# Issuing the first batch's Newton products twice and moving up the first output products in a fused attention and gated-network kernel

## The chip, the core and the metric

The kernel runs on one core of a Trainium2 chip. The metric is device time in microseconds (us) of one execution, in runs of one program; less is better. A core has TensorE (PE, with its weight loads as a separate row, PEld), VectorE (DVE), ScalarE (ACT), GpSimd (POOL) and the queue of SyncE (SP), which here issues nearly all loads. Matmul results land in PSUM, which has eight banks.

## What is computed

Nyström attention over 4 batches, 8 heads, 576 rows and 64 columns, then two gated layers (512 to 1536 to 512) over the 2304 rows. Cut to what matters:

```python
q_lm, k_lm = means of 18 consecutive rows: 32 landmarks per head
A, Bm, C = softmax(q k_lm^T), softmax(q_lm k_lm^T), softmax(q_lm k^T)
Z = Bm.T / (norm1(Bm) * norminf(Bm) + 1e-6)
for _ in range(6):
    Z = 2 * Z - Z @ Bm @ Z            # Newton rounds, 32x32 per head
x = A @ Z @ C @ v
g = x @ w_gate; x = (g * sigmoid(g) * (x @ w_val)) @ w_out     # layer 1
x = (sigmoid(x @ w_gate2) * (x @ w_val2)) @ w_out2             # layer 2
```

## The kernel before

The attention output is never formed. For each batch b, `front(b, g)` (g is one half of the heads) takes the landmark means (`lm`), transposes k and q on TensorE (`tp`, `lt`), and forms the three softmaxes (`cs` and `e` for C, `bm` and `bs` for Bm, `as` and `sx` for A) and C·v (`cv`). `back(b)` normalises Bm and runs the Newton rounds. A round is eight products of 32x32 by 32x96, one for each head, made by `prod` (L273 to L278) into the tile `nw`, and one update on DVE (L283 for the first round, L288 for five, L294 for the last), which makes the next `rw`. After seven such products the result is transposed (`ut`, L297) and copied to `UT`.

Layer 1 goes over six chunks c of 256 hidden columns. `uw_steps` (word U) multiplies `UT[b]` by the chunk's gate and value weights (`pu`), and splits the result into two parts (`uw`, L360 on ACT, L361 on DVE). `gv1_steps` (word G) multiplies that by A (`pg`, `pv`), applies SiLU on ACT (L453), multiplies on DVE (L455), and splits again (`hh`, `hl`). `o1_steps` (word O) multiplies by the output weights (`po`); for c = 0 the sum is copied by ACT (`acc`, L479), later it is added by DVE (L481). Layer 2 follows, from about 620 us on.

The weights come in as raw 32-bit pieces (`raw`, three buffers, loaded by SP in order with the loads of q, k and v). Each piece is converted by two ACT instructions (L324, L327) and two DVE instructions (L329, L333); an output piece (`wo`) also takes a cast on ACT (L360) and a subtraction on DVE (L361). A chunk has four pieces for gate and value and two for the output.

The order in which this is written out is a list of words, `first` (L589 to L592). F, B, U, G and O are the steps above; `I0` and `I1` convert chunk 0 or 1 up to its fourth piece, which U needs; `J0` and `J1` go on to its sixth, which O needs. While a U, G or O word is written out, the weight conversion advances by one step after each of its steps. The framework's scheduler then sets each engine's queue, with the written order as priority, so that instructions of neighbouring words mix. Each engine works through its queue strictly in that order. ACT loads a table (ACT_TABLE_LOAD) each time it changes between the exponentials of a front and SiLU.

PSUM has four groups of banks: `gv` 3, `n` 1 (`nw`, `ut`), `o` 2, `a` 2. The matmuls of `nw` write one bank.

Of the kernel before, what the change touches and what calls it, by code (L numbers as in the profile page):

```python
# [14 lines left out]
def nystrom_moe_kernel(tc, q, k, v, wg1, wv1, wo1, wg2, wv2, wo2, out):  # L15
    nc = tc.nc
    B, H, S, D = q.shape
    M = 32
    P = 128
# [23 lines left out]
    def ptile(shape, tag, name):  # L43
        return psum.tile(shape, F32, tag=tag, name=name, bufs=PB[tag])
# [16 lines left out]
    def mm(o, l, r, start=True, stop=True):  # L61
        nc.tensor.matmul(o, l, r, start=start, stop=stop, skip_group_check=True)  # L62
# [19 lines left out]
    def flat(x):  # L82
        return x.rearrange("p a b -> p (a b)")
# [6 lines left out]
    def step(fill, n=1):  # L90
        while n and fill:
            try:
                next(fill[0])
                n -= 1
            except StopIteration:
                fill.pop(0)
# [4 lines left out]
    def small(tag, shape, nm_, bufs=2):  # L101
        return att.tile(shape, F32, tag=tag, name=f"{tag}{nm_}", bufs=bufs)

    def pst(b, shape, nm, g=0):

        tag = "n" if nm in ("nw", "ut") else "a"
        if b == 0:
            tag = {"tp": "gv", "cs": "o", "as": "o"}.get(nm, tag)
        return ptile(shape, tag, f"{nm}_{b}_{g}")
# [113 lines left out]
    def a_steps(b, g):  # L223
        s = SX[b, g]
        asm = small("asm", [P, L], f"{b}_{g}")
        nc.vector.tensor_reduce(asm, s, axis=AX.X, op=ALU.add)
        nc.vector.tensor_scalar(asm, asm, 1e-9, None, op0=ALU.add)
        nc.vector.reciprocal(asm, asm)
        yield
        nc.vector.tensor_tensor(s, s, asm[:, :, None].to_broadcast([P, L, M]), op=ALU.mult)  # L230
        yield
        at = flat(small("sx", [P, L, M], f"{b}_{g}t", 3))
        nc.vector.transpose(out=at, in_=flat(s))
        hi, lo = AH[:, 8 * g + b], AH[:, 8 * g + 4 + b]
        nc.scalar.copy(hi, at)
        nc.vector.tensor_tensor(lo, at, hi.bitcast(F32), op=ALU.subtract)
        AT[b, g, 0] = hi
        AT[b, g, 1] = lo
        yield

    def back(b):

        def sm(tag, shape, bufs=2):
            return small(tag, shape, b, bufs)

        bs, bsm, BC = BS[b]

        nc.vector.tensor_scalar(bsm, bsm, 1e-9, None, op0=ALU.add)
        nc.vector.reciprocal(bsm, bsm)
        nc.vector.tensor_tensor(bs, bs, bsm[:, :, None].to_broadcast([P, 2, M]), op=ALU.mult)  # L250
        nc.scalar.copy(BC[:, :, 0:M], bs)

        bmt = sm("bmt", [P, 2, M])
        nc.vector.transpose(out=flat(bmt), in_=flat(bs))
        nrm = sm("nrm", [P, 2, 2])
        nc.vector.tensor_reduce(nrm[:, 0], bs, axis=AX.X, op=ALU.add)
        nc.vector.tensor_reduce(nrm[:, 1], bmt, axis=AX.X, op=ALU.add)
        yield
        nb = sm("nb", [P, 4, M], 1)
        nc.vector.tensor_copy(nb, nrm.rearrange("p a b -> p (a b)")[:, :, None].to_broadcast([P, 4, M]))  # L260
        nbt = sm("nbt", [P, 4, M], 1)
        nc.vector.transpose(out=flat(nbt), in_=flat(nb))
        nmax = sm("nmax", [P, 2, 2])
        nc.vector.tensor_reduce(flat(nmax), nbt, axis=AX.X, op=ALU.max)
        rr = sm("rr", [P, 2])
        nc.vector.tensor_tensor(rr, nmax[:, 0], nmax[:, 1], op=ALU.mult)
        nc.vector.tensor_scalar(rr, rr, 1e-6, None, op0=ALU.add)
        nc.vector.reciprocal(rr, rr)
        yield


        def prod(x):
            ps = pst(b, [P, 2, 96], "nw")  # L273
            for g in range(2):
                for h in range(4):
                    hs = slice(M * h, M * h + M)
                    mm(ps[hs, g], x[hs, g, 0:M], x[hs, g])
            return ps  # L278

        ga = [a_steps(b, g) for g in range(2)]  # L280
        ps = prod(BC)
        RW = sm("rw", [P, 2, 96], 2)
        nc.vector.tensor_tensor(RW, ps, rr[:, :, None].to_broadcast([P, 2, 96]), op=ALU.mult)  # L283
        yield
        for it in range(5):
            ps = prod(RW)
            RW2 = sm("rw", [P, 2, 96], 2)
            nc.vector.scalar_tensor_tensor(RW2, RW, 2.0, ps, op0=ALU.mult, op1=ALU.subtract)  # L288
            RW = RW2
            step(ga)  # L290
            yield
        ps = prod(RW)
        UU = flat(sm("rw", [P, 2, 96], 2))[:, 0:P].rearrange("p (g d) -> p g d", g=2)
        nc.vector.scalar_tensor_tensor(UU, RW[:, :, M:], 2.0, ps[:, :, M:], op0=ALU.mult, op1=ALU.subtract)  # L294
        yield
        ps = pst(b, [P, P], "ut")
        nc.tensor.transpose(ps, flat(UU), ident)  # L297
        nc.vector.tensor_copy(flat(UT[b]), ps)
        yield
        while ga:  # L300
            step(ga)
            yield
# [273 lines left out]
    def emit(word, nw=1):  # L576
# [10 lines left out]

    wfill.extend(weights(0, c) for c in range(2))
    first = (  # L589
        "F00 F01 B0 I0 F10 U00 G00 J0 F11 I1 U10 B1 O00 G10 J1 F20 O10 U01 G01 "  # L590
        "F21 U11 B2+F30 O01 G11 F31 U02 O11 G02 B3 U12 O02 G12 U03 O12 G03 U13 O03 G13"
    )  # L592
    for w in first.split():
# [78 lines left out]
```

## Time and profile before

| | us |
|---|---|
| median of 3 runs | 907.71 (906.84 to 910.90) |
| profiled execution | 907.64 |
| its span, first to last instruction | 905.9 |
| TensorE busy | 872.2 (96%), mean granted clock 0.991 |
| VectorE busy | 523.4 (58%) |
| ScalarE busy | 396.3 (44%) |
| TensorE busy in the first 110 us | 84.47, mean granted clock 0.92 |

The profiled execution is 0.07 us under the median. A granted clock of 1.00 is 2.4 GHz, of 0.50 is 1.2 GHz; a stretch with a value between holds both. Busy shares over the whole span say little here: the last three quarters are bound by TensorE, and what can be lost or won lies in the first 110 us, where fronts, Newton rounds and weight conversions compete for all engines.

### The profile page before, as it was taken

The page shows a single profiled execution, that of the slowest core. Times are in us where ns is not written, and L with a number is a line of the kernel's source. Part 1 is how long each engine was busy: PE and PEld are TensorE (multiplying, and loading weights), DVE is VectorE, ACT ScalarE, POOL GpSimd, SP SyncE. Part 2 cuts the span into 40 slices and gives each one's busy share as a digit, 9 for nine tenths or more (in the row PEclk, how much of TensorE's full clock was granted, in tenths as well). Part 3 has the DMA queues.
Part 4 walks back from the last instruction along what each step waited for, and adds up shares of the span by engine and source line. Part 5 has one row for each costly group of instructions (what it writes and reads, how often), then busy time and mean ns, then how long its engine had stood idle before and what let it go on. Part 6 is the DMA issues. An engine that isn't in the chain of part 4 may idle for free.

```text
span 905.9 us, 16181 instructions
## 1 busy us (share of the span) xinstructions
PE 872.2 (96%) x6604; PEld 744.0 (82%) x6604; DVE 523.4 (58%) x1079; ACT 396.3 (44%) x845; POOL 55.8 (6%) x90
## 2 busy tenths in 40 slices
PE   5778999999999999999999999999999999999997
PEld 4456777789999999999988888888888888888886
DVE  4977665765977678769861153355347236433342
ACT  5688477755653355537643262143125114111111
POOL 4530323000000000000000000000000000000000
PEclk9898999999999999999999999999999999999999
DMA  8666221011611132203010031012004000000132
GB/s 270 178 201 195 80 78 30 3 52 43 177 52 52 48 94 71 71 4 114 24 47 1 1 101 39 1 52 88 1 1 139 1 1 24 1 1 0 47 94 71
DMA packets 27083, 57.68 MB, mean 64 GB/s; under 512 B 4224, under 2 KB 7296, under 8 KB 27008
## 3 DMA queue, kind: packets, MB, share of 16 engines
q1 hardware_dynamic: 25280, 54.28, 20.1%
q10 hardware_dynamic: 1728, 2.36, 1.1%
q8 instruction: 52, 0.85, 0.4%
q14 instruction: 23, 0.19, 0.1%
HBM read 51.90 MB, written 4.72 MB: 63 GB/s over the span
## 4 chain that ended last, share of the span: by engine, by line
PE 89%; DVE 4%; ACT 4%; issue 1%; DMA 1%; SPq 0%; ACTq 0%; DVEq 0%
PE po L62 33%; PE pv L62 24%; PE pg L62 24%; PE pu L62 3%; PE tp L145 1%; PE nw L62 1%; PE cs L62 1%; ACT L453 1%; DMA raw<-in_moe_w_val_dram 1%; PE as L62 1%; PE cv L62 1%; DVE lm L131 0%; DMA kin<-in_k_dram 0%; ACT e L172 0%; PE et L195 0%
## 5 line engine op out<-in xcount | busy, mean ns | idle before, releaser
L62 PE MATMUL po<-hh,wo 128*128 128x288 f32 x768 | 164.9, 303 | 1.4 <-ACT acc L479 0.9
L62 PE MATMUL po<-wo,h 128*128 128x512 f32 x648 | 152.2, 389 | 0.0
L526 DVE TENSOR_TENSOR hf<-hf,pv 128x512 f32<-128x512 f32 (+1 forms) x60 | 38.1, 634 | 194.2 <-PE pv L62 194.2
L62 PEld LDWEIGHTS po<-wo,h 128*128 128x128 f32 x648 | 121.1, 188 | 25.3 <-ACT h L360 0.3
L62 PEld LDWEIGHTS po<-hh,wo 128*128 128x128 f32 x768 | 124.4, 188 | 17.1 <-issue 12.9
L62 PE MATMUL pg<-AH,w 128*128 128x512 f32 (+1 forms) x480 | 136.1, 368 | 0.0
L62 PE MATMUL pv<-AH,w 128*128 128x512 f32 (+1 forms) x480 | 136.0, 368 | 0.0
L62 PE MATMUL po<-hl,wo 128*128 128x288 f32 x384 | 113.5, 297 | 0.0
L525 ACT ACTIVATE hf<-pg 128x512 f32<-128x512 f32 (+1 forms) x60 | 33.2, 553 | 165.7 <-PE pg L62 152.1
L62 PE MATMUL pg<-AH,uw 128*128 128x288 f32 x576 | 100.0, 299 | 0.5 <-ACT uw L360 0.5
L62 PE MATMUL pv<-AH,uw 128*128 128x288 f32 x576 | 97.6, 300 | 2.6 <-ACT sg L453 2.6
L62 PEld LDWEIGHTS pg<-AH,w 128*128 128x128 f32 x480 | 87.3, 188 | 15.5
L62 PEld LDWEIGHTS pv<-AH,w 128*128 128x128 f32 x480 | 87.0, 189 | 15.0
L360 ACT CAST h<-hf 128x512 fp32r<-128x512 f32 (+1 forms) x60 | 34.6, 576 | 124.2 <-DVE hf L526 124.2
L62 PEld LDWEIGHTS pg<-AH,uw 128*128 128x128 f32 x576 | 83.7, 188 | 5.5 <-issue 3.4
L62 PEld LDWEIGHTS pv<-AH,uw 128*128 128x128 f32 x576 | 83.3, 190 | 5.6 <-ACT sg L453 3.1
L547 DVE TENSOR_TENSOR oacc<-po,oacc 128x512 f32<-128x512 f32 x90 | 61.9, 691 | 41.0 <-PE po L62 39.9
L62 PE MATMUL pg<-x1l,w 128*128 128x512 f32 x192 | 74.7, 389 | 0.0
L62 PE MATMUL pv<-x1l,w 128*128 128x512 f32 x192 | 74.7, 389 | 0.0
L62 PEld LDWEIGHTS po<-hl,wo 128*128 128x128 f32 x384 | 72.2, 188 | 0.7 <-DVE uw L361 0.5
L481 DVE TENSOR_TENSOR acc<-po,acc 128x288 f32<-128x288 f32 x128 | 56.4, 454 | 16.1 <-PE po L62 15.6
L324 ACT ACTIVATE cv<-raw 128x512 f32<-128x512 f32 x72 | 48.5, 674 | 26.5 <-DVE cv L333 11.3
(121 smaller groups left out, 1092.1 us busy)
## 6 DMA issues: line engine op xcount, KB each, us to landing
raw<-in_moe_w_out_dram SPq DMA_DIRECT2D x24, 512.0 KB, 4.0
raw<-in_moe_w_gate_dram SPq DMA_DIRECT2D x48, 128.0 KB, 3.2
raw<-in_moe_w_val_dram SPq DMA_DIRECT2D x48, 128.0 KB, 3.2
raw<-in_moe_w_gate_dram SPq DMA_DIRECT2D x24, 256.0 KB, 3.0
raw<-in_moe_w_val_dram SPq DMA_DIRECT2D x24, 256.0 KB, 3.4
kin<-in_k_dram SPq DMA_DIRECT2D x8, 576.0 KB, 4.4
qin<-in_q_dram SPq DMA_DIRECT2D x8, 576.0 KB, 5.5
vin<-in_v_dram SPq DMA_DIRECT2D x8, 576.0 KB, 5.5
```

What stands on the lines that cost most here:

```text
L62: nc.tensor.matmul(o, l, r, start=start, stop=stop, skip_group_check=True)
L145: nc.tensor.transpose(ps[:, j], flat(src[:, 2 * u:2 * u + 2]), ident)
L324: nc.scalar.activation(t0, hiw.bitcast(F32), AF.Copy, scale=2.0 ** -112)
L360: nc.scalar.copy(hi, x)
L453: nc.scalar.activation(sg, pss[0], AF.Silu)
L481: nc.vector.tensor_tensor(sl, ps, sl, op=ALU.add)
L525: nc.scalar.activation(h, pss[0], AF.Sigmoid)
L526: nc.vector.tensor_tensor(h, h, pss[1], op=ALU.mult)
L547: nc.vector.tensor_tensor(acc, ps, acc, op=ALU.add)
```

## The change

Two things. First, for batch 0 `prod` issues its eight products twice, the second time into further columns of the same `nw` tile (five groups of 96 columns wide, within one bank), which nothing reads. Second, in the list of words `F11`, `J0` and `O00` move ahead of `B1` and `I1`.

```diff
         def prod(x):
-            ps = pst(b, [P, 2, 96], "nw")
-            for g in range(2):
-                for h in range(4):
-                    hs = slice(M * h, M * h + M)
-                    mm(ps[hs, g], x[hs, g, 0:M], x[hs, g])
-            return ps
+            ps = pst(b, [P, 5 if b == 0 else 2, 96], "nw")
+            for o in range(0, 4 if b == 0 else 2, 2):
+                for g in range(2):
+                    for h in range(4):
+                        hs = slice(M * h, M * h + M)
+                        mm(ps[hs, o + g], x[hs, g, 0:M], x[hs, g])
+            return ps[:, 0:2]
...
-        "F00 F01 B0 I0 F10 U00 G00 J0 F11 I1 U10 B1 O00 G10 J1 F20 O10 U01 G01 "
+        "F00 F01 B0 I0 F10 U00 G00 F11 J0 O00 B1 I1 U10 G10 J1 F20 O10 U01 G01 "
```

In the built programs TensorE's semaphore is raised once for each round, on its last product: after the eighth before, after the sixteenth now. The update on DVE waits for that, so for batch 0 it now stands behind the second eight products as well.

On TensorE, the Newton rounds of batch 0 stand among the transposes and `cs` products of the next batch's front. Before:

```order
L62 MATMUL nw_0_476<-rw_474 32x96 x8
L145 MATMUL tp_0_667<-ident,qin_0_147 128x128 x3
L145 MATMUL tp_0_672<-ident,qin_0_147 128x128 x3
L62 MATMUL nw_0_491<-rw_485 32x96 x8
L145 MATMUL tp_0_677<-ident,qin_0_147 128x128 x3
L62 MATMUL cs_0_691<-kq_0_635,bdq_0_663 32x288
L62 MATMUL nw_0_503<-rw_500 32x96 x8
```

Now, at the same place on TensorE:

```order
L62 MATMUL nw_0_484<-rw_482 32x96 x16
L135 MATMUL lt_0_717<-ident,lm_0_709 128x128
L145 MATMUL tp_0_723<-ident,qin_0_147 128x128 x3
L62 MATMUL nw_0_507<-rw_501 32x96 x16
L145 MATMUL tp_0_728<-ident,qin_0_147 128x128 x3
L145 MATMUL tp_0_733<-ident,qin_0_147 128x128 x3
L62 MATMUL cs_0_747<-kq_0_691,bdq_0_719 32x288
L62 MATMUL nw_0_527<-rw_524 32x96 x16
```

Each round has sixteen products, and three transposes moved from ahead of the third round to behind it.

On ACT, from the casts of the first `uw` to the first SiLU of G00 (`pg` to `sg`, behind its table load). Before:

```order
L360 CAST uw_0_0_817<-pu_0_0_803 128x512
L196 COPY eT_0_718<-et_0_719 96x384
L360 CAST uw_0_1_821<-pu_0_1_804 128x512
L184 ACTIVATE bs_684,bsm_685<-bs_684 128x32
L196 COPY eT_0_718<-et_0_724 96x384
L327 ACTIVATE cv_855<-raw 128x512
L324 ACTIVATE cv_935<-raw 128x512
L327 ACTIVATE cv_936<-raw 128x512
L360 CAST wo_0_564<-cv_855 128x512
L453 ACT_TABLE_LOAD
L453 ACTIVATE sg_0_0_841<-pg_0_0_827 128x288
```

Now, from the same front's `bs` exponential on:

```order
L184 ACTIVATE bs_740,bsm_741<-bs_740 128x32
L196 COPY eT_0_774<-et_0_775 96x384
L196 COPY eT_0_774<-et_0_780 96x384
L362 CAST wo_0_620<-cv_675 128x512
L326 ACTIVATE cv_991<-raw 128x512
L362 CAST uw_0_0_873<-pu_0_0_859 128x512
L362 CAST uw_0_1_877<-pu_0_1_860 128x512
L362 CAST wo_0_620<-cv_911 128x512
L329 ACTIVATE cv_992<-raw 128x512
L455 ACT_TABLE_LOAD
L455 ACTIVATE sg_0_0_897<-pg_0_0_883 128x288
```

The front's exponential and copies and one weight conversion moved ahead of the `uw` casts; behind them, ahead of the table load, stand two instructions where there were six.

On TensorE, from the last product of G00 on (`pv_0_0_911` before, `pv_0_0_967` now): the transposes of F11, then before:

```order
L145 MATMUL tp_1_994<-ident,qin_1_328 128x128 x3
L62 MATMUL cs_1_1005<-kq_1_952,bdq_1_980 32x288 x4
L62 MATMUL cs_1_1011<-kq_1_952,bdq_1_980 32x288 x4
L62 MATMUL pu_0_1_1156<-w_1_933,ut_82 32x512
L62 MATMUL pu_0_0_1155<-w_1_933,ut_82 32x512
```

And now:

```order
L145 MATMUL tp_1_1045<-ident,qin_1_328 128x128 x3
L62 MATMUL po_0_0_1193<-hh_0_0_901,wo_0_620 128x288 x2
L62 MATMUL po_0_0_1193<-hl_0_0_902,wo_0_620 128x288
L145 MATMUL tp_1_1050<-ident,qin_1_328 128x128 x3
L62 MATMUL cs_1_1061<-kq_1_1008,bdq_1_1036 32x288 x4
L62 MATMUL po_0_0_1193<-hh_0_0_932,wo_0_620 128x288
L62 MATMUL cs_1_1067<-kq_1_1008,bdq_1_1036 32x288 x4
L62 MATMUL po_0_0_1193<-hh_0_0_932,wo_0_620 128x288
L62 MATMUL po_0_0_1193<-hl_0_0_933,wo_0_620 128x288
L62 MATMUL po_0_0_1211<-hh_0_0_901,wo_0_620 128x288 x2
```

The products of U10 (`pu`), which need four converted pieces of chunk 1, stood right behind F11's `cs`; now all 48 `po` products of O00, the rest of F11 and the first Newton round of batch 1 stand ahead of them. The last 4382 of TensorE's 5662 products have the same order in both programs.

## Rows read from the trace of the kernel before

**Rows 1.** Busy time by stretch of the span; columns in the first line.

```profile
core 0: us, PE busy (x) PEld busy (x) DVE busy (x) ACT busy (x) POOL busy (x), PEclk, DMA share, GB/s
28.60:32.00 3.40, 1.59 (x9) 0.98 (x9) 3.40 (x7) 2.31 (x6) 3.09 (x6) 1.00 1.03 263
32.00:38.60 6.60, 5.89 (x63) 3.49 (x67) 6.23 (x11) 4.79 (x11) 5.33 (x7) 0.50 0.46 139
38.60:44.60 6.00, 3.06 (x63) 1.42 (x63) 5.89 (x14) 3.03 (x5) 0.00 (x0) 0.98 0.44 138
57.90:62.70 4.80, 4.78 (x25) 4.40 (x25) 3.67 (x8) 3.95 (x11) 0.82 (x2) 0.65 0.42 115
62.70:70.25 7.55, 3.20 (x26) 1.32 (x26) 5.10 (x9) 5.97 (x13) 4.49 (x6) 0.95 0.82 281
70.25:76.40 6.15, 6.15 (x67) 3.35 (x71) 3.22 (x8) 5.47 (x15) 0.00 (x0) 0.50 0.58 172
76.40:86.30 9.90, 8.95 (x160) 8.08 (x156) 9.07 (x29) 7.15 (x17) 0.00 (x0) 1.00 0.76 186
57.90:88.20 30.30, 24.98 (x283) 19.06 (x284) 22.66 (x55) 24.22 (x55) 5.31 (x8) 0.83 0.67 193
86.30:97.20 10.90, 10.20 (x146) 8.28 (x145) 8.12 (x16) 5.50 (x12) 4.01 (x6) 1.00 0.19 57
97.20:210.00 112.80, 109.44 (x1455) 89.23 (x1452) 74.80 (x193) 77.45 (x170) 19.52 (x32) 1.00 0.20 57
210.00:620.00 410.00, 410.00 (x2737) 366.43 (x2737) 260.18 (x542) 192.06 (x414) 0.00 (x0) 1.00 0.19 57
```

**Rows 2.** Who TensorE waited for, 26 to 100 us: total, times, longest.

```profile
PE pu L62 <- DVE w L333: 4.6, 2, 3.5
PE pv L62 <- ACT sg L453: 2.1, 1, 2.1
PE po L62 <- ACT acc L479: 0.9, 1, 0.9
```

**Rows 3.** TensorE in order of time: start, us, instruction, [idle before <-releaser].

```profile
32.71 0.86 PE L62 MATMUL nw<-rw 32*32 32x96 f32 x16 [1.91 <-DVE rw L283]
...
37.70 0.86 PE L62 MATMUL nw<-rw 32*32 32x96 f32 x16
38.49 1.31 PE L62 MATMUL cs<-kq,bdq 128*32 128x288 f32 x14
...
42.27 0.53 PE L62 MATMUL nw<-rw 32*32 32x96 f32 x16 [1.00 <-DVE rw L288]
43.22 0.33 PE L297 MATMUL ut<-ident,rw 128*128 128x128 f32 x1 [0.41 <-DVE rw L294]
44.62 1.09 PE L62 MATMUL pu<-w,ut 64*32 64x512 f32 x16 [1.08 <-DVE w L333]
...
90.17 0.53 PE L62 MATMUL nw<-rw 32*32 32x96 f32 x16
90.63 0.93 PE L62 MATMUL pg<-AH,uw 128*128 128x288 f32 x5
```

**Rows 4.** ACT in order of time, same columns.

```profile
46.86 0.60 ACT L360 CAST uw<-pu 128x512 fp32r<-128x512 f32 x1
...
50.08 0.69 ACT L327 ACTIVATE cv<-raw 128x512 uint32<-128x512 uint32 x1
51.31 0.62 ACT L360 CAST wo<-cv 128x512 fp32r<-128x512 f32 x1 [0.54 <-DVE cv L333]
51.94 1.28 ACT L453 ACT_TABLE_LOAD   x1
53.24 0.41 ACT L453 ACTIVATE sg<-pg 128x288 f32<-128x288 f32 x1
...
57.93 0.41 ACT L453 ACTIVATE sg<-pg 128x288 f32<-128x288 f32 x1
...
88.21 0.41 ACT L453 ACTIVATE sg<-pg 128x288 f32<-128x288 f32 x1
```

## The prediction, before the result was known

> **What bounds the kernel now.** I read the busy time by stretch first. From 210 to 620 us TensorE is busy in all of 410.00 us, and from 97 to 210 us in 109.44 of 112.80 at full clock [rows 1]. So whatever TensorE has gained or lost when it gets there stays to the end, as long as the work behind is the same; the last 4382 of its products stand in the same order in both programs. The case is decided ahead of 97 us.
>
> There the reader should see three losses. From 32 to 38.6 us the clock is at 0.50, that is 1.2 GHz, while TensorE is busy for 5.89 of 6.60 us [rows 1]; this is the Newton stretch of batch 0. From 62.7 to 70.25 us TensorE is busy for 3.20 of 7.55 us, and the longest wait of all lies there: `pu` of U10 waits 3.5 us for the last piece of chunk 1's weights (`w`, L333) [rows 1, 2]. Then from 70.25 to 76.4 us it works without a gap, but at 0.50 [rows 1]. Over 57.9 to 88.2 us, from one SiLU of G00 to the first of G10, TensorE is busy 24.98 us at a mean clock of 0.83, ACT 24.22 and DVE 22.66, of 30.30 [rows 1, 4]. No engine is full: 24.98 x 0.83 is 20.7 us of TensorE work at full clock, so some 9.6 us are lost to waits and to the low clock.
>
> **Part 1, the doubled products.** Eight products take 0.79 us from their start to that of the next work at the low clock (37.70 to 38.49) and 0.46 at the full one (90.17 to 90.63) [rows 3]. The added ones do not run beside the update of their own round, since it waits for the sixteenth product. So a round gets longer by one of these two times. The first is free: its products end before 28 us, and its update (`rw`, L283) comes only just ahead of 32.71, behind other DVE work [rows 3]. Rounds 2 to 4 fall in the low-clock stretch, 5 to 7 behind it: 3 x 0.79 + 3 x 0.46 = 3.8 us on the way to `ut`, if nothing hides it. Some of it is hidden: DVE is busy for 6.23 of 6.60 and 5.89 of 6.00 us there, and the late rounds waited for it (1.00 and 0.41 us) [rows 1, 3]. That DVE work can run while the second eight run, as far as the queue's order lets it. The least is therefore 3.8 - 1.4 = 2.4 us. I take 2.6, nearer to the low end, because DVE was full. `ut` then starts at 45.8 instead of 43.22, and `pu` of U00, which waited for weights until 44.62 and not for `ut` [rows 3], starts at about 46.5: 1.9 late.
>
> Who waits for that? G00's first SiLU. Before, the first `uw` cast starts at 46.86 and the table load only at 51.94, because six instructions stood between the second cast and the load, among them a `wo` cast that waited 0.54 us for DVE [rows 4]. Now `pu` ends at 46.5 + 1.1 = 47.6; ACT ends a conversion (until 48.3), makes two `uw` casts (0.5 each), a `wo` cast (0.6), a conversion (0.7, of the 0.69 in [rows 4]) and the load (1.28): 51.9 us, against 53.24. I take -1.2 us at G00's SiLUs, since the second SiLU follows through the same two table loads. Bounds: -2.5 (all of the lateness hidden) and +1 (`pu` 3.8 late and a DVE wait on top).
>
> **Part 2, the moved words.** The 48 `po` products of O00 now come into the wait for chunk 1's weights, and U10 comes behind them. TensorE's wait of 3.5 us for `w` goes, and the 0.9 us that `po` waited for an `acc` copy [rows 2] becomes a wait among other work. What is next? ACT. Its work of the stretch is the same but for the ends: two `kq` copies and two `bdk` scalings come in ahead of G10's first SiLU, and one pair of conversions (2 x 0.69 [rows 4]) goes behind it, which I take as equal. So ACT's 24.2 us [rows 1] is the floor, 6.1 under the 30.3 of before. It won't be reached: the exponentials of F11 and the `bm` product, whose bank they free, still follow each other, and the last `uw` cast waits for `pu`. I give these 1.2 us, half of what the same kind of waits on TensorE's side comes to in [rows 2] (2.1). That makes -4.9 us; bounds -6.1 (ACT never waits) and -2 (two thirds of its waits stay, which were for copies and transfers and not for `pu`).
>
> SP matters here as well: in the new order the second `val` load of chunk 1's fourth piece stands ahead of F11's `kin` load and not behind it, so it no longer queues behind a load that waits for transposes. I cost this at nothing; it is part of why the `w` wait goes.
>
> At G10's first SiLU the new order has run four Newton rounds of batch 1 where the old one has run one, and some five more transposes, with four `pv` and `pg` products left over. Transposes and products are alike in time (0.93 us for five products [rows 3], so below 0.2 each): 3 x 0.46 and one product more, 1.5 us less to do. TensorE is busy 10.20 of 10.90 us from 86.3 on [rows 1], so nearly all of it counts: -1.5; bounds 0 and -2.5.
>
> **The sum.** -1.2 - 4.9 - 1.5 = -7.6 us, against the profiled execution's 907.64, which is 0.07 under the median: 900.0 us. The bounds together, +1 - 2 + 0 and -2.5 - 6.1 - 2.5, give 906.6 and 896.5.
>
> **A rule on the clock.** TensorE ran transposes and one product of two columns from 28.6 to 32.0 us, 1.59 of 3.40 us, and the clock was at 0.50 behind it; from 38.6 to 44.6 us it was busy for about the same share, 3.06 of 6.00, with Newton and `cs` products among it, and the clock stayed at 0.98 [rows 1]. The Trainium skill, "TensorE: Matmul & The Clock Gate", Part 1 (the clock gate), says that the low clock is the default and that activity of the engine releases it. By that rule the second eight products, which fill gaps with activity, should bring the clock up sooner in the Newton stretch; the rows agree in that the clock did come back after a busy stretch, and do not show whether so few more products are enough.
>
> **The rivals.**
> Clock back early, as a mechanism of this kernel: the added products lift the clock at the third round instead of behind the fourth. Two rounds of sixteen then take 0.92 instead of 1.58 us each, and half of the low-clock `cs` time (1.31 us [rows 3]) is saved: 1.3 + 0.7 = 2.0 us. For it: the two rows above. Against: in 32.0 to 38.6 us TensorE was busy for nine tenths and the clock still came back only at the end [rows 1], and no added product falls into the stretch of transposes ahead of 32 us. Time: 898.0.
>
> ACT keeps its waits: eight `acc` copies stand in ACT's queue among F11's copies, and each that waits for a `po` holds up the conversions of chunk 1 behind it. Then the wait for `w` is replaced by one for `acc`, and part 2 brings 2 us in all: 907.6 - 1.2 - 2 = 904.4. For it: ACT was idle 6.1 us in the stretch, of which the profile puts little down to `pu`. Against: TensorE would be well ahead of ACT there, so that an `acc` copy finds its product done.
>
> Slower, by the clock: with O00 used up early, TensorE has nothing to do while ACT works through F11's exponentials (about 66 to 69 us). The clock falls to 1.2 GHz there, and if TensorE, waiting for ACT in between, isn't busy enough to get it back, U10, the Newton rounds of batch 1 and G10 run at 0.50. What ran from 76.4 to 97.2 us (8.95 + 10.20 us at 1.00 [rows 1]) would take up to 19 us more; 12 of them would put the kernel at 912. It decides from about 12 us of added low clock in work that bounds, since before had 6 us of it (70.25 to 76.4) already. Against: at 70.25 to 76.4 us TensorE was full and the clock did come back [rows 1]; low clock makes TensorE busier, and so ends itself.
>
> **How the numbers follow.** Forecast 0.68 (900.0, own range 896.5 to 904), clock back early 0.09 (898.0), ACT keeps its waits 0.15 (904.4), slower by the clock 0.08 (912). A measurement of this kernel can tell about 0.5% from no change, that is 4.5 us: faster is below 903.2. Of the forecast's 0.68 some 0.64 lie below it, of the third case's 0.15 a third: 0.64 + 0.09 + 0.05 = 0.78. Slower is the last case, 0.08; the rest, 0.14, is no change. The range 895.5 to 905.0 leaves out the slower case and the edges, about 0.18.
>
> **What the profile of the changed kernel should show.** `ut` at 45 to 47 us; the update of a round starting behind 32 matmul records; clock at 0.50 from about 32 to 39 us as before. First SiLU of G00 at 51 to 53 us. No idle time over 1 us on TensorE ahead of `pu` of U10, and ACT the fullest engine from 57 to 82 us. First SiLU of G10 at 81 to 83 us, instead of 88.21. The stretch from 210 us on unchanged in length. I am wrong if G10's first SiLU comes later than 85 us (part 2), if G00's comes behind 54 us (part 1), or if it comes early and TensorE shows new gaps or a low clock between there and 210 us.

## The result, and the profile after

The changed kernel takes 901.11 us (median of 4 runs, 899.44 to 901.30) against 907.53 for the kernel before on the same chip (906.84 to 910.90): a ratio of 0.9913, 95% interval 0.9894 to 0.9932. On a second chip it took 900.74 against 908.49, 0.9908 (0.9891 to 0.9924). The forecast of 900.0 and its range hold. Its terms do not hold as well, as the lines below begin to show. The profiled execution is the 899.44 one, 1.7 us under the median, with a mean granted clock of 0.997 where the other eight runs on the two chips have 0.993 to 0.995; its span is 897.6 us against 905.9.

The stretches of after that answer to [rows 1] (us of the stretch, then busy us of PE, PEld, DVE, ACT and POOL with instruction counts, granted clock, DMA share, GB/s):

```profile
32.00:38.60 6.60, 5.33 (x122) 3.46 (x122) 6.54 (x11) 4.71 (x11) 5.96 (x9) 1.00 0.60 168
38.60:44.60 6.00, 3.89 (x115) 2.65 (x110) 5.96 (x17) 4.89 (x11) 0.00 (x0) 1.00 0.59 183
54.90:84.40 29.50, 24.42 (x336) 18.63 (x336) 23.68 (x57) 23.53 (x56) 10.56 (x15) 0.94 0.66 188
69.00:77.80 8.80, 8.17 (x194) 5.94 (x193) 8.19 (x22) 8.44 (x20) 2.53 (x4) 1.00 0.80 189
77.80:80.30 2.50, 0.72 (x20) 0.34 (x17) 2.50 (x6) 0.17 (x1) 2.26 (x3) 1.00 0.80 212
80.30:83.70 3.40, 3.40 (x31) 2.85 (x28) 2.98 (x7) 1.76 (x2) 0.00 (x0) 0.51 0.10 36
97.00:202.00 105.00, 101.83 (x1400) 84.20 (x1398) 70.86 (x185) 72.92 (x161) 15.18 (x26) 1.00 0.18 50
202.00:612.00 410.00, 410.00 (x2738) 366.42 (x2737) 260.12 (x542) 191.99 (x414) 0.00 (x0) 1.00 0.18 57
```

The clock never fell in the Newton stretch of this execution (1.00 where [rows 1] have 0.50). From 54.90 to 84.40, from the third SiLU of G00 to the first of G10, ACT is busy 23.53 of 29.50 us, so it is idle 5.97, as much as before. A hole lies at 77.80 to 80.30 us: TensorE busy for 0.72 and ACT for 0.17 of 2.50 us, DVE for all of it. The low clock of 80.30 to 83.70 follows that hole. From 202 us on TensorE is full again, so everything was decided earlier.

Who TensorE waited for, 26 to 100 us (total, times, longest), against [rows 2]:

```profile
PE nw L62 <- DVE rw L290: 4.8, 6, 1.8
PE bm L62 <- ACT e L172: 1.5, 1, 1.5
PE as L62 <- DVE bc L203: 1.2, 2, 0.9
PE lt L135 <- ACT kq L146: 0.8, 1, 0.8
```

The 3.5 us that `pu` of U10 waited for weights are gone, as is the wait of `pv` for SiLU. Waits for the Newton update stand in their place, the longest with 1.8 us.

TensorE in the Newton stretch, against [rows 3] (start, us, instruction; x32 are the records of sixteen products):

```profile
39.44 0.86 PE L62 MATMUL nw<-rw 32*32 32x96 f32 x32 [0.50 <-DVE rw L290]
41.27 0.86 PE L62 MATMUL nw<-rw 32*32 32x96 f32 x32 [0.97 <-DVE rw L290]
42.62 0.86 PE L62 MATMUL nw<-rw 32*32 32x96 f32 x32 [0.49 <-DVE rw L290]
43.42 0.27 PE L62 MATMUL bm<-bdk,bdq 128*32 128x32 f32 x8
...
44.06 0.30 PE L299 MATMUL ut<-ident,rw 128*128 128x128 f32 x1
...
44.94 1.09 PE L62 MATMUL pu<-w,ut 64*32 64x512 f32 x16
```

ACT, against [rows 4]:

```profile
46.73 1.04 ACT L362 CAST uw<-pu 128x512 fp32r<-128x512 f32 x2
...
48.91 1.28 ACT L455 ACT_TABLE_LOAD   x1
50.21 0.41 ACT L455 ACTIVATE sg<-pg 128x288 f32<-128x288 f32 x1
...
80.72 0.48 ACT L146 COPY kq<-tp 128x384 f32<-128x384 f32 x1 [2.76 <-PE tp L145]
81.22 1.28 ACT L455 ACT_TABLE_LOAD   x1
84.48 0.41 ACT L455 ACTIVATE sg<-pg 128x288 f32<-128x288 f32 x1 [1.97 <-PE pg L62]
```

`ut` comes 0.84 us later than before and `pu` 0.32, yet G00's first SiLU comes 3.03 us earlier, since its table load stands two instructions behind the casts. G10's first SiLU comes 3.73 us earlier. ACT's two waits ahead of it, 2.76 and 1.97 us, are 4.73 of its 5.97 us of idle time.

What DVE did in the hole, then POOL:

```profile
76.30 1.99 DVE L236 TENSOR_TENSOR AH<-sx_0t,AH 128x576 fp32r<-128x576 f32 x1
78.21 0.69 DVE L227 TENSOR_SCALAR asm<-asm 128x18 f32<-128x18 f32 x1
78.82 0.68 DVE L331 SCALAR_TENSOR_TENSOR cv<-cv,cv 128x512 uint32<-128x512 uint32 x1
79.42 0.34 DVE L290 SCALAR_TENSOR_TENSOR rw<-rw,nw 128x192 f32<-128x192 f32 x1
...
86.65 0.75 DVE L236 TENSOR_TENSOR AH<-sx_1t,AH 128x576 fp32r<-128x576 f32 x1
```

```profile
76.26 1.42 POOL L124 TENSOR_TENSOR ls<-kin 128x576 f32<-128x576 f32 x1
77.75 1.11 POOL L125 TENSOR_TENSOR ls<-ls 128x256 f32<-128x256 f32 x1
...
86.67 2.00 POOL L124 TENSOR_TENSOR ls<-qin 128x576 f32<-128x576 f32 x1
```

The same subtraction (L236) takes 0.75 us at 86.65 and 1.99 at 76.30, where POOL had begun a landmark sum 0.04 us ahead of it: it ends 0.61 us behind that sum. At 86.65 the subtraction began first, by 0.02 us, and there it is POOL's sum that takes 2.00 us instead of 1.42. The Newton update (L290) waits behind the held-up subtraction in DVE's queue, the next round's products wait for the update, the transposes and `pg` products for those, and ACT for them.

### The profile page after: what moved, and what is told of

It reads as the page before. It is cut to its first block, busy times and chain, and to the rows that moved or that the text cites. A ratio compares the mean times of both kernels' runs of the same rounds, so it can differ in the third digit from the quotient of the medians.

```text
span 897.6 us, 16406 instructions
## 1 busy us (share of the span) xinstructions
PE 867.7 (97%) x6716; PEld 743.6 (83%) x6716; DVE 522.8 (58%) x1079; ACT 395.6 (44%) x845; POOL 56.6 (6%) x90
## 4 chain that ended last, share of the span: by engine, by line
PE 89%; DVE 5%; ACT 4%; issue 1%; DMA 0%; ACTq 0%; DVEq 0%
PE po L62 34%; PE pv L62 25%; PE pg L62 24%; PE pu L62 2%; PE tp L145 1%; PE nw L62 1%; PE cs L62 1%; PE as L62 0%; DVE lm L131 0%; DMA kin<-in_k_dram 0%; DVE cv L331 0%; ACT cv L326 0%; DVE hl L363 0%; DVE asm L226 0%; ACT e L172 0%
## 5 line engine op out<-in xcount | busy, mean ns | idle before, releaser
L62 PEld LDWEIGHTS pg<-AH,uw 128*128 128x128 f32 x576 | 83.7, 189 | 5.1 <-issue 3.6
```

## The experiments

All times are medians, all ratios are to the kernel before on the same chip. The SiLU times are of the profiled execution of each.

| kernel | first SiLU of G00 | third of G00 | first of G10 | span | time | ratio (95%) |
|---|---|---|---|---|---|---|
| before | 53.24 | 57.93 | 88.21 | 905.9 | 907.5 to 909.8 | 1 |
| changed | 50.21 | 54.91 | 84.48 | 897.6 | 901.11 | 0.9913 (0.9894 to 0.9932) |
| changed, again | 49.98 | 54.67 | 85.31 | 898.9 | 900.74 | 0.9908 (0.9891 to 0.9924) |
| doubled products alone | 50.15 | 54.84 | 82.87 | 899.6 | 901.64 | 0.9924 (0.9905 to 0.9943) |
| moved words alone | 54.94 | 59.63 | 86.54 | 899.9 | 900.71 | 0.9910 (0.9889 to 0.9931) |
| second eight behind the update | 55.49 | 60.18 | 90.58 | 904.1 | 905.74 | 0.9964 (0.9946 to 0.9982) |
| changed order, second eight narrow | 50.90 | 55.59 | 84.54 | 897.8 | 900.97 | 0.9915 (0.9898 to 0.9931) |
| words alone, wide products | 55.50 | 60.20 | 86.62 | 900.1 | 902.13 | 0.9926 (0.9911 to 0.9940) |
| changed, k sums left out | 50.70 | 55.39 | 84.90 | 897.8 | 900.73 | 0.9914 (0.9892 to 0.9937) |
| changed, k sums cut in place | 50.35 | 55.04 | 82.54 | 895.9 | 896.47 | 0.9863 (0.9843 to 0.9883) |
| changed, two landmark tiles | 49.31 | 55.06 | 85.32 | 899.3 | 901.26 | 0.9916 (0.9901 to 0.9931) |
| changed, sums in three | 49.33 | 54.02 | 81.00 | 893.9 | 897.42 | 0.9874 (0.9855 to 0.9893) |
| words alone, sums in three | 51.47 | 56.16 | 81.38 | 895.2 | 896.88 | 0.9865 (0.9843 to 0.9887) |
| before, sums in three | 52.40 | 57.09 | 86.95 | 903.3 | 905.34 | 0.9960 (0.9944 to 0.9977) |

**Each change alone.** The first kernel has only the first of these edits to the kernel before, the second only the second.

```diff
-            for g in range(2):
+            for o in range(0, 4 if b == 0 else 2, 2):
+                for g in range(2):
...
-                    mm(ps[hs, g], x[hs, g, 0:M], x[hs, g])
+                        mm(ps[hs, o + g], x[hs, g, 0:M], x[hs, g])
```

```diff
-        "F00 F01 B0 I0 F10 U00 G00 J0 F11 I1 U10 B1 O00 G10 J1 F20 O10 U01 G01 "
+        "F00 F01 B0 I0 F10 U00 G00 F11 J0 O00 B1 I1 U10 G10 J1 F20 O10 U01 G01 "
```

> The doubled products alone, with the words in the order of before. Theory A (the added products keep TensorE's clock up from 32 to 38.6 us, and that pays for them): clock 1.00 there, `ut` at about 44, first SiLU of G00 at 50.2 us as in the changed kernel, 3.0 ahead of 53.24. Then the wait of `pu` of U10 for the weights of chunk 1 stays, since the words are the old ones, and moves along or not: 904.5 us if the loads come 3 us earlier too, 907 if they do not. Rival B (the clock stayed up for another reason, and each doubled round costs 0.46 to 0.79 us): clock 0.50 from 32 to 38.6 us, `ut` at 45 to 46, first SiLU of G00 at 52 to 54, and 907 to 910 us.

> The moved words alone, with single products. Theory A: clock 0.50 from 32 to 38.6 us as before, `ut` at 43.2, first SiLU of G00 at 53 us or, if the moved words alone take instructions out from ahead of the table load, at 52; no wait of `pu` of U10; G10's first SiLU about 3 us later than the 84.48 of the changed kernel, and 904 us. Rival B (the words bring everything, the products only cost): 899 to 901 us, with G10's first SiLU at 84.5 or earlier.

Each alone brings the whole gain (901.64 and 900.71 us), so the two are not the independent terms that the forecast added up. With the doubled products alone G00's first SiLU comes 3.1 us early, as in the changed kernel, and the wait for chunk 1's weights stays but is shorter (2.4 us against 3.5 in [rows 2]):

```profile
PE pu L62 <- DVE w L335: 2.4, 1, 2.4
```

and the stretch of 70.25 to 76.40 us, at 0.50 in [rows 1], is at 0.94:

```profile
70.25:76.40 6.15, 6.15 (x148) 5.60 (x147) 5.83 (x16) 6.09 (x15) 0.00 (x0) 0.94 0.68 172
```

Both theories had it slower, since neither let the lead at G00 grow (it is 5.3 us at G10). With the words alone, G00 comes 1.7 us late, and the low clock lies elsewhere:

```profile
44.60:52.00 7.40, 7.00 (x95) 4.15 (x99) 5.07 (x12) 6.15 (x15) 0.00 (x0) 0.50 0.61 207
```

In that time its `pu` takes 1.96 us instead of the 1.09 of [rows 3]. Rival B had the time right and the way there wrong: this execution loses 1.7 us up to G00 and has 6.0 at the end.

**The products or the order?** Writing the products twice also makes the scheduler set ACT's and DVE's queues anew, presumably since it takes TensorE to be busy for longer. To part the two, the built program was edited behind the scheduler, so that all queues keep their order. In one kernel (narrow) the second eight products of the changed order are cut to 2 columns; in the other (wide) the eight products of the words-only order are doubled in width.

```diff
+    # behind the scheduler, for each second product of batch 0 (32x96)
+    outs, ins = 32x2 of the output, 32x2 of the moving operand
```

```diff
+    # behind the scheduler, for each product of batch 0 (32x96, single)
+    outs, ins = 32x2x96: the second 96 columns 192 further on, the moving operand read twice
```

> The changed kernel with every queue in exactly its order, but the second eight products of each round of batch 0 cut to 2 columns each. It parts the columns that TensorE works through from the order that the scheduler gave ACT and DVE. Theory O (the new order on ACT, with the table load two instructions behind the `uw` casts, is what brings G00's first SiLU forward): it comes at 49.5 to 50.5 us again, whatever the clock does. Theory K (the columns keep the clock up, and that is what brings it forward): the clock is at 0.50 in part of 32 to 39 us, `ut` comes at 44.5 or later, the first SiLU at 51.5 to 53 us. If the low clock moves on to G00 as in the kernel with the moved words alone (0.50 from 44.6 to 52 us), 903 to 904 us; without it 899.5 to 901.

> The kernel with the moved words alone, every queue in exactly its order, but each of the eight products of a round of batch 0 twice as wide: 192 columns, the second 96 of them again into columns that nothing reads. Theory K: clock 1.00 from 32 to 44.6 us and none of the low clock that the words alone showed from 44.6 to 54 us; G00's first SiLU at 51.5 to 52.5 us instead of 54.94, and 898 to 899.5 us. Theory O: the old order on ACT keeps it at 53 us or later, and 900 to 902 us, since the wider products only cost (3 to 6 rounds by 0.2 us) in a stretch that DVE paces.

What brings G00 forward is the order. In the narrow kernel's profiled execution, with next to no added columns, the clock is low through the whole Newton stretch:

```profile
28.60:32.00 3.40, 2.56 (x10) 1.72 (x10) 3.40 (x8) 2.07 (x6) 3.16 (x5) 0.55 1.05 255
32.00:38.60 6.60, 5.73 (x84) 4.12 (x88) 5.91 (x12) 5.02 (x13) 4.57 (x5) 0.50 0.52 151
```

`pu` starts at 45.63 instead of 44.94, G00's first SiLU comes at 50.90 instead of 50.21 (between what the two theories gave, and nearer to theory O), and the median is 900.97, that of the changed kernel. Nor is most of the gain the clock of the whole run: at a mean granted clock of 0.991 the kernel before took 906.80 us on this chip, and four runs of the narrow kernel 899.63 to 901.10. Over the runs the added columns do raise the clock: the mean granted clock was 0.990 to 0.992 in six runs of the narrow kernel and 0.993 to 0.997 in nine of the changed one. They cost about what this brings, since the medians agree. In the old order the wide products bring no earlier SiLU (55.50 us) and 902.13 us, 1.4 above the words alone, which the intervals can't tell apart.

**Beside the update, as intended.** The changed kernel's update waits for all sixteen products. Here the second eight are written out behind the update.

```diff
+        def again():
+            if b == 0:
+                eight(last[0], last[1], 2)
...
         nc.vector.tensor_tensor(RW, ps, rr[:, :, None].to_broadcast([P, 2, 96]), op=ALU.mult)
+        again()
```

> The changed kernel, but each round's second eight products are written behind the update that the first eight feed, so that the update waits for its own eight alone. Price of the wait: six rounds by 0.2 (eight products at full clock) to 0.46 us are 1.2 to 2.8 us earlier at `ut`, first SiLU of G00 at 47.5 to 49, and 898 to 900 us if it is kept. Rival (the rounds are paced by DVE's queue, so the update would not have run sooner): `ut` at 44 within 0.5 us, and 901. Third case: the second eight, now free of the round, run at other moments and the clock falls again: 0.50 somewhere from 32 to 39 us, and 903 to 904.

It loses most of the gain, 905.74 us. Two of the late rounds:

```profile
43.68 1.15 PE L62 MATMUL nw<-rw 32*32 32x96 f32 x32 [0.48 <-DVE rw L300]
45.51 1.15 PE L62 MATMUL nw<-rw 32*32 32x96 f32 x32 [0.68 <-DVE rw L300]
```

The second eight of a round now start only when the update is done, together with the next round's first eight, and they stand ahead of these in TensorE's queue. `ut` comes at 47.81 us, 3.75 later than in the changed kernel. Of these, 0.97 are there at the first update (32.49 against 31.52 us), 1.62 come in the next three rounds, with the clock at 0.50 from 32.0 to 38.6 us, 0.44 in the last three, and 0.72 between the last update and `ut`, where further products stand ahead of it. Of the three cases, the third is nearest; how much is the clock and how much the queue was not parted.

**The hole ahead of G10.** Four kernels take POOL's work away from there, or try to.

```diff
-            if (b, g) > (0, 0):
+            if (b, g) == (2, 1) and which == "k":
+                for w in range(2):
+                    nc.gpsimd.tensor_tensor(lm[:, w], src[:, 0], src[:, 1], op=ALU.add)
+            elif (b, g) > (0, 0):
```

> The changed kernel without the landmark means of one half of one later batch: the k sums of batch 2, second half, are left out (two short adds stand in their place), which takes POOL's work away at 76 to 80 us, and a part of the result with it. Theory C (DVE's addition at line 236 took 1.99 us instead of 0.75 because POOL summed beside it, and the Newton round and the kq copies behind it waited): line 236 takes 0.7 to 0.8 us there, TensorE has no wait of over 1 us from 77.8 to 80.3 us, the clock stays at 1.00 there, G10's first SiLU comes at 81 to 82.5 us instead of 84.48, and the time is 898 to 899 us. Rival D (DVE is full there anyway, 2.50 of 2.50 us, and the addition only shows it): G10's first SiLU within 0.7 us of 84.48, and 901.

This one told nothing: with the k sums gone, the q sums behind them in POOL's queue moved up into the same place (76.70 us), and the subtraction took 1.98 us as before. The second buffer for the landmark tile did the same from the other side:

```diff
-            lm = sm("lm", [P, 2, D], 1)
+            lm = sm("lm", [P, 2, D], 2)
...
```

> The changed kernel with the tile of landmark means in two buffers, so that POOL's next sums need not wait for the transpose of the last ones and run at 65 to 69 us, ahead of the stretch where DVE is full (three small tiles go from two buffers to one for the space). Theory C: line 236 takes 0.75 us, no wait of TensorE over 1 us at 78 to 80 us, G10's first SiLU at 82 to 83 us, 898 to 899.5 us. Rival D: no change, 901. Rival E (POOL's sums disturb DVE wherever they are, and at 65 to 69 us DVE was busy too): some of the gain is lost there, 900 to 901.

The k sums ran earlier, the q sums came to stand at 77.50 us, the subtraction took 2.00 us, and the time stayed at 901.26. So the sums were cut short in place, behind the scheduler:

```diff
+    # behind the scheduler, the four sums (L124 to L127) of the k landmarks of batch 2, second half
+    576, 256, 128, 64 columns -> 128, 2, 2, 2
```

> The changed kernel with every queue in exactly its order, but POOL's sums for the k landmarks of batch 2, second half, cut short in place (576, 256, 128 and 64 columns become 128, 2, 2 and 2), so those landmark means are left out. In the run before, taking them out let the q sums move up into their place, and POOL was as busy as ever. Theory C (POOL's work beside it stretches DVE's addition at line 236 from 0.75 to 1.99 us and the tiny step at line 227 from 0.14 to 0.69): both are short again at 76 to 79 us, TensorE's wait of 1.8 us for the Newton update goes below 0.7, the clock stays at 1.00 at 80 to 84 us, G10's first SiLU comes at 81.5 to 83 us, and 898 to 899.5 us. Rival D (DVE's queue is full there anyway): 84.0 to 84.5 us and no change, 901.

Theory C holds, though the subtraction keeps 1.03 us beside what is left of the sums. DVE, TensorE and ACT in that place:

```profile
77.33 1.03 DVE L238 TENSOR_TENSOR AH<-sx_0t,AH 128x576 fp32r<-128x576 f32 x1
78.29 0.16 DVE L229 TENSOR_SCALAR asm<-asm 128x18 f32<-128x18 f32 x1
```

```profile
79.37 0.53 PE L62 MATMUL nw<-rw 32*32 32x96 f32 x16 [0.30 <-DVE rw L292]
```

```profile
82.54 0.41 ACT L457 ACTIVATE sg<-pg 128x288 f32<-128x288 f32 x1 [0.56 <-PE pg L62]
```

The subtraction (here L238) is 0.96 us shorter, the tiny step behind it 0.53, TensorE's wait 1.48 (0.30 instead of 1.78); the clock stays at 1.00 from 80.3 to 83.7 us, and G10's first SiLU comes 1.94 us earlier. ACT's two waits ahead of it are 1.20 and 0.56 us, so 2.97 of the 4.73 us went with the sums. The narrow kernel splits this further: its subtraction takes 1.99 us and ACT's first wait 2.80 as in the changed kernel, but its clock stays at 1.00 behind the hole, and ACT's second wait is 0.56 instead of 1.97. The time is 896.47 us, a ratio lower by 0.0045 to 0.005 than that of the changed kernel, some 4 us: more than the 1.9 of the profiled executions, in which the changed kernel's was its fastest and this kernel's its slowest. What the rest is was not traced.

**A version that keeps the result.** If the subtraction waits for the end of the POOL instruction that began before it, shorter POOL instructions must help with nothing left out. This run was made with the changed kernel, with the words alone, and with the kernel before; the changed kernel itself ran beside the first two.

```diff
-                nc.gpsimd.tensor_tensor(x, src[:, 0:NU], src[:, NU:], op=ALU.add)
+                for u in range(0, NU, 3):
+                    us = slice(u, u + 3)
+                    nc.gpsimd.tensor_tensor(x[:, us], src[:, us], src[:, NU + u:NU + u + 3], op=ALU.add)
```

> The changed kernel once more, beside the next two on one chip, so that their times compare directly: 900.5 to 901.5 us, line 236 at 1.9 to 2.0 us, G10's first SiLU at 84 to 85 us.

> The changed kernel with POOL's first landmark sum (576 columns, 1.41 us) written as three sums of 192 columns, every other queue in exactly its order and the whole result computed. Theory L (a DVE instruction with two operands in SBUF waits for the POOL instruction that began before it, to its end): line 236 waits for one third at most and takes 0.9 to 1.4 us instead of 1.99, G10's first SiLU comes 0.6 to 1.1 us earlier than in the changed kernel, other collisions in the first 110 us shrink as well, and 898.5 to 900 us. Theory B (POOL's work slows DVE by its amount, as a shared bandwidth would): three sums take some 0.5 us more in all than one, line 236 stays at 1.8 to 2.2, and 901 to 902 us.

> The moved words alone, single products, with POOL's first landmark sum in three pieces. Line 236 took 1.90 us beside POOL there too (80.74 us). Theory L: 1.3 us or less, and 898.5 to 900 us, at least 0.7 under the 900.7 of the words alone. Theory B: 900.5 to 901.5.

> The kernel before with POOL's first landmark sum in three pieces, every other queue in exactly its order and the whole result computed. Before shows four places where a DVE instruction is long beside POOL: the steps of 2 columns at 23.58 us (1.25 instead of 0.16) and 29.20 us (1.32), line 227 at 34.16 us (1.13), and line 236 at 89.73 us (1.56). Theory N (the wait that cost the changed kernel most, at line 236 ahead of G10, came with the moved words): the pieces bring before 1 to 2 us only, 907 to 908.5 us. Rival G (such waits cost the same everywhere): 3 to 4 us as in the changed kernel, 904.5 to 906 us, and then part of what the changed order gained can be had without it.

Theory L holds and theory B does not. In the changed kernel with the sums in three:

```profile
75.27 1.17 DVE L238 TENSOR_TENSOR AH<-sx_0t,AH 128x576 fp32r<-128x576 f32 x1
76.35 0.57 DVE L229 TENSOR_SCALAR asm<-asm 128x18 f32<-128x18 f32 x1
```

```profile
75.22 2.74 POOL L126 TENSOR_TENSOR ls<-kin 128x192 f32<-128x192 f32 x3
```

POOL's three take 2.74 us beside DVE where one took 1.42, and still DVE's subtraction falls from 1.99 to 1.17 and the time by 3.3 us against the changed kernel on the same chip. That is more than theory L gave, and G00's first SiLU already comes 0.65 to 0.88 us earlier, so other such waits shrank too. The changed kernel beside it has its first SiLU of G10 at 85.31 us, a little behind what was expected. The words alone with the sums in three have the lowest median of the kernels that leave nothing out: 896.88 us (896.28 to 897.19), below all runs of the changed kernel beside it (899.86 to 901.14), but not told apart from the changed kernel with the sums in three (895.73 to 899.11). Its stretch from the third SiLU of G00 to the first of G10:

```profile
56.10:81.40 25.30, 23.05 (x326) 17.55 (x330) 19.36 (x50) 22.91 (x57) 11.37 (x20) 1.00 0.64 188
```

The kernel before gains from it too, 905.34 against 909.71, as rival G said and theory N did not. Such waits were spread over its first 100 us: `ut` comes at 41.38 us instead of 43.22 there. So such waits are not something that the change made. The moved words did bring one to the subtraction ahead of G10: it takes 0.75 us in the kernel before (at 81.69) and with the doubled products alone (at 76.58), and 1.90 to 2.00 us in the kernels with the moved words and whole sums.

## Why the prediction was right, and where it was not

**The sum was right by luck: three errors nearly cancelled.** The terms were -1.2, -4.9 and -1.5 us. In the profiled execution they are -3.0 (G00's first SiLU), -0.7 (third SiLU of G00 to first of G10: 29.57 against 30.28 us) and -4.6 (from there to the end: 813.1 against 817.7). In the repeat they are -3.3, +0.4 (30.64 us) and -4.1 (813.6). The middle term, the largest, all but failed, and the other two made up for it.

**The signs.** ACT as the fullest engine, the rounds of 32 records and the unchanged stretch at the end came as forecast. `ut` (44.06 us), G00's first SiLU (50.21) and G10's (84.48) lie outside their ranges, the low clock of 32 to 39 us did not come, and TensorE did wait for over 1 us ahead of U10's `pu` (1.5 us, `bm` for an exponential). The repeat's first SiLU of G10, at 85.31, is past the 85 us that the prediction had named as its proof against part 2.

**Part 1** named the right mechanism: from the start of `pu` to the first SiLU it went from 8.62 to 5.27 us, 3.35 less, where the working had 3.1. What failed is the step that let six longer rounds put `ut` 2.6 us and `pu` 1.9 us late. `ut` was 0.84 late and `pu` 0.32; in the repeat, whose clock was at 0.71 and 0.89 in the Newton stretch, 0.59 and 0.08. So it wasn't the clock alone. From the first products on `rw` to `ut` the rounds took 12.15 us, in the repeat 11.53, against 10.51 before: 1.0 to 1.6 us more, not 2.6. An added eight cost 0.34 us at the full clock (0.80 from 42.62 to 43.42, less the 0.46 of eight products), not 0.46. And these products began 0.80 and 0.43 us earlier (31.91 and 32.28 against 32.71 us), where the working took the first round to change nothing. The first rival, "clock back early", is in the changed kernel's trace in a stronger form, since the clock never fell there. The narrow kernel shows what it is worth: 0.7 us at G00 and nothing in the median. The rule that the prediction took from the Trainium skill, "TensorE: Matmul & The Clock Gate", Part 1, that activity releases the low clock, agrees with these runs in the mean (0.990 to 0.992 without the columns, 0.993 to 0.997 with them, in one order). Single traces do not show it: from 32.0 to 38.6 us the clock was at 0.50 (before), 0.74 (words alone) and 1.00 (the kernel before and the words alone, each with the sums in three) without added columns, and at 0.50 (second eight behind the update) to 1.00 with them. The working counted the new order on ACT within this part; the kernels edited behind the scheduler show that it does most of it (2.34 of the 3.03 us).

**Part 2** named the right wait and the right next limit. The 3.5 us of `pu` went, and ACT was to be the floor, with 1.2 us left to wait. ACT was idle for 5.97 us, 4.73 of them in two waits behind one subtraction on DVE, of which 2.97 went when the sums were cut. The step that failed is "I give these 1.2 us": it asked what ACT waits for in the old order and not which instructions of DVE and POOL the new order puts side by side. (Half of 2.1 is 1.05 and not 1.2, which changes nothing here.) Without that wait the stretch is 27.50 us (sums cut), 26.98 (sums in three) and 25.22 (words alone, sums in three), that is -2.8, -3.3 and -5.1. The term of -4.9 is reached once neither POOL's long sums nor the doubled products stand in the way.

Here a rule of the Trainium skill was missed that bears on this part. "SBUF — State Buffer", section "SBUF: two separate sides", says that VectorE and GpSimd share one port pair under an exclusive lock, and that a DVE operation with two inputs in SBUF and a GpSimd operation hold it for a whole instruction each. The runs agree: the subtraction takes 0.75 us alone, 1.99 beside a sum of 1.42 and 1.17 beside sums of a third, and the sum 2.00 where the subtraction began first.

**Part 3**, the work already ahead, was undersized: -4.6 against -1.5 with a bound of -2.5. From G10's first SiLU to the stretch in which TensorE is full, before and then after:

```profile
88.21:210.00 121.79, 117.73 (x1583) 95.60 (x1581) 81.32 (x206) 81.27 (x180) 23.53 (x38) 1.00 0.19 56
84.48:202.00 117.52, 113.98 (x1529) 94.25 (x1527) 81.12 (x206) 81.72 (x179) 19.72 (x32) 1.00 0.21 59
```

TensorE is busy for 3.75 us less and idle for 0.52 less; the remaining 0.3 us lie behind. At that SiLU the kernel before still had six Newton rounds of batch 1 and nine transposes of `kin` to do, the changed one two rounds, most of a third, and one transpose. In these stretches the rounds come to 1.6 us less (8.7 against 10.3), the transposes of `kin` to 1.4 less (4.8 against 6.2), and the `pg` and `pv` products to the same (47.4 against 47.5). So the step that failed is the one that let five transposes cancel against four products; in the runs eight of them counted in full. Some 0.75 us of the busy time, spread over other products, was not traced further.

**The other rivals.** "ACT keeps its waits" came true in its number (ACT's idle time is the same) but not in its mechanism, since no wait for an `acc` copy is among TensorE's longer ones. "Slower, by the clock" did not come. In the profiled execution the low clock shrank to 3.4 us, from 80.3 to 83.7. In the repeat it did fall where this rival had it (0.82 from 62.70 to 70.25 us), but it was back at 0.94 in the next 6.15 us.

**Open.** Why the two parts together bring no more than either alone is shown only in part. With the moved words the wait for POOL takes back some 2 us ahead of G10, with the doubled products alone it does not; yet with the sums in three the words alone (0.9865) are still as good as both together (0.9874). That the doubled products then only cost, as in the wide kernel, fits, but the difference is within the intervals. And whether the doubled products with the old words gain by their order or by their columns was not run: the narrow kernel has the moved words too.

## What to carry to other kernels

Where a scheduler sets the queues, adding work changes the order of everything near it: test the order without the work, and the work without the order, before crediting either. Ahead of moving work between stages, look at which two-operand DVE instructions will run beside long POOL instructions, and cut the POOL instructions into pieces; here that was worth 3.3 to 4.4 us in three kernels, about half as much as the change itself. Extra TensorE work raised the mean clock here and paid just for itself.

## What was not expected of the hardware

A DVE instruction of 128x18 elements took 0.69 us instead of 0.16 beside POOL, so even the smallest steps are held up, and the profile counts this as busy time: DVE looked full (2.50 of 2.50 us) while it waited.

The granted clock of one program differs from execution to execution. Of fifteen runs of the kernel before on one chip, seven had a mean clock of 0.982 and took 910.04 to 911.09 us; the three with 0.991 to 0.993 took 905.65 to 907.16. One trace's low stretches are therefore one draw: a repeat of the changed kernel showed 0.71 from 28.6 to 32.0 us and 0.89 from 32.0 to 38.6, where the first showed 1.00 in both.
